# Real 2-D Fourier mixing and a sigmoid-GELU feed-forward block on one core: the Nyquist broadcast issued earlier, and VectorE's and ScalarE's work of a step in another order

## The chip, the cores and the metric

The kernel runs on one core of one Trainium2 chip. The metric is the device time of one execution in microseconds (us), of which lower is better. Before the change the median of three executions is 2043.21 us (2042.82 to 2043.45).

## The reference

```python
x        : (8, 3008, 256) float32            # batch, sequence, width
X        = fft(fft(x, axis=1), axis=2).real   # "FNet" mixing: only the real part is kept
t        = X.reshape(8 * 3008, 256)
h        = t @ w_in                           # w_in  (256, 2048)
g        = h * (1 / (1 + exp(-1.702 * h)))    # quick GELU
out      = g @ w_out                          # w_out (2048, 256)
```

The kernel folds the transform over the width (256 columns) into `w_in` once at the start. The transform over the sequence, 3008 = 47 x 64, is done in two stages on TensorE. Because the input is real, the rows come in pairs: for a frequency and its mirror image the hidden values are P + Q and P - Q (up to one column, the Nyquist column, which adds a term N of its own). So TensorE makes P and Q once and two rows of hidden values come out of them.

## The kernel before

Each batch has three blocks of frequencies, each block two halves, each half eight steps; a step takes 256 hidden units (two groups `i` of 128) for 256 (in one half of the first block 226) pairs of rows. That is 48 steps per batch and 384 in all. The first eight are treated in a simpler way; all others run through the loop below. Counted within a batch, steps 0 to 15 are block 0, 16 to 31 block 1, 32 to 47 block 2.

The loop is software-pipelined. "Step t" is one turn of it, and works on several steps at once:

```python
for t in range(n + LAG):                      # LAG = 3
    ...
    else:                                     # t >= NP = 8
        if t < n:
            if t + 2 < n:
                middle(t + 2)                 # ScalarE: g = af2 * nb            (N, needs the Nyquist broadcast)
            second(t)                         # TensorE: x[t] += Q               4 matmuls of 64 columns each
        product(t - LAG, 0)                   # TensorE: 2 of 7 output products
        if t + 1 < n:
            begin(t + 1)                      # TensorE: x[t+1] = P
        product(t - LAG, 1)                   # TensorE: the other 5 products
        ...
        if t < n:
            forward(t)                        # ScalarE: h[forward half] = gelu(x)
        sums(t - 2, nc.vector)                # VectorE: s2, s4
        if t < n:
            backward(t)                       # VectorE: h[reversed half] = g - x  (rows reversed)
            activate_back(t)                  # ScalarE: gelu of the reversed half, in place
            sums(t, nc.gpsimd)                # GpSimd:  s1, s3
    if NP <= t + 1 < n:
        doubled(t + 1)                        # VectorE: g = 2 P + N   (must be read before second(t+1) adds Q)
    ...
    if t >= LAG:
        combine(t - LAG)                      # every eighth step: finish an output block
        ...
    if t >= NP:
        spare[:] = ["b2", f"b{t % 2}"]        # PSUM banks that side work may take
    for fn, args in extra.get(t, ()):         # side work of this step, at its end
        fn(*args)
```

`x` lies in one of two PSUM banks, `b0` and `b1`, by the parity of its step. The side work borrows bank `b2` and the bank of the step that has just been turned back.

```python
def doubled(t):
    n = width(t)
    g = two(gt[t][:], n)
    nc.vector.scalar_tensor_tensor(g, two(xb[t][:], n), 2.0, g, op0=ALU.mult, op1=ALU.add)

def backward(t):
    reversed_sum(t, gt.pop(t), xb.pop(t), ALU.subtract)

def sums(t, eng):                             # h = a11, a12, a21, a22: forward 0, 1, reversed 0, 1
    ...
    if eng is nc.gpsimd:
        eng.tensor_tensor(s1, a21, a22, op=ALU.add)
        eng.tensor_tensor(s3, a11, a21, op=ALU.subtract)
    else:
        eng.tensor_tensor(s2, s1, a11, op=ALU.subtract)
        eng.tensor_tensor(s4, a12, s2, op=ALU.subtract)
```

The output products are a Strassen-Winograd scheme: seven products in place of eight, accumulated over the eight steps of a half in four PSUM banks `pot[0]`, `pot[1]`, `pot[2]` and `pot[5]`. `deep(t)` is always False in this kernel, so the parts that are guarded by it do nothing.

```python
# product(t, part): the first two of plan are part 0, the rest part 1
plan = [(0, 0, wo[:, p, 0, :], h[:, 0, 0, :n]), (0, 1, wt[:, p, 1, :], s[:, 1, :n]),
        (1, 0, wt[:, p, 2, :], s[:, 2, :n]), (1, 1, wt[:, p, 0, :], s[:, 0, :n]),
        (2, 0, wo[:, p, 3, :], s[:, 3, :n])]
if not deep(t):
    plan += [(2, 1, wo[:, p, 2, :], h[:, 0, 1, :n]), (5, 0, wt[:, p, 3, :], h[:, 1, 1, :n])]
```

After the eighth step `combine` adds the seven accumulated products up, turns the result and stores it:

```python
nc.scalar.copy(c1, pot[0][:, 0:n])
plan = [(u2, c1, m[6], ALU.add), (u3, u2, m[7], ALU.add), (u2, u2, m[5], ALU.add), (c22, u3, m[5], ALU.add),
        (c12, u2, m[3], ALU.add)]
...
plan = [*plan[:1], (c11, c1, m2, ALU.add), plan[1], plan[2], plan[4], plan[3], (c21, u3, m4, ALU.subtract)]
for out_, i0, i1, how in plan:
    nc.vector.tensor_tensor(out_, i0, i1, op=how)
    ...
for half in range(2):
    turned(t, o, half, c[:, 2 * half:])       # VectorE transpose, then four stores
```

Of the side work four kinds matter here. For every block but the first, `stage2` makes the block's `pq` (P's and Q's moving operand) in step 8 of the block before it, and `nyquist` copies the Nyquist column of `pq` to all 128 partitions by a DMA. For the next batch `fold1` (GpSimd) and `mix1` (TensorE) make the first stage in pieces, `spill` and `fill` send it through device memory, and `turn` and `load_x` bring in a later batch.

```python
def nyquist(b, blk):
    nb = nbt[b, blk] = pqp.tile([128, 512], F32, tag="nb", name="nb")   # two buffers
    row = pqt[b, blk][0:1, 1, :]
    if (b, blk) != (0, 0):
        nc.sync.dma_start(out=nb[:], in_=free(row, 0, [0, 128], [1, 512]))
        return
    ...

for b in range(B):
    t0 = b * NBLK * NF
    late = 0 if b else 3
    if b + 2 < B:
        at(t0 + 10, turn, b + 2)
    if b + 1 < B:
        for c in range(NCH):
            at(t0 + 7 + 2 * c + late, fold1, b + 1, c, nc.gpsimd)
            if c % 2:
                at(t0 + 8 + 2 * c + late, mix1, b + 1, c // 2)
        at(t0 + 24 + late, spill, b + 1)
        at(t0 + 29 + late, fill, b + 1)
        ...
    for blk in range(NBLK):
        nxt = (b, blk + 1) if blk + 1 < NBLK else (b + 1, 0)
        if nxt[0] < B:
            at(t0 + blk * NF + 8, stage2, *nxt)
            at(t0 + blk * NF + 12, nyquist, *nxt)
```

The first use of a block's broadcast is `middle(t + 2)` of the block's first step, and so stands at the head of step 14 of the block before. In the first batch GpSimd also prepares differences of the output weights (`differences`, `small_weights`) in steps 7 to 12.

Of the kernel before, what the change touches and what calls it, by code (L numbers as in the profile page):

```python
# [27 lines left out]
F32 = mybir.dt.float32  # L28
U32 = mybir.dt.uint32
ALU = mybir.AluOpType  # L30
# [13 lines left out]
LAG = 3  # L44
# [6 lines left out]
def free(ap, offset, *dims):  # L51
    return bass.AP(ap.tensor, ap.offset + offset, [list(ap.ap[0])] + [list(d) for d in dims])
# [59 lines left out]
def kernel(ctx: ExitStack, tc, x, w_in, w_out, tab1, tab2, out):  # L112
# [324 lines left out]
    def differences(n):  # L437
        ps = slice(2 * n, 2 * n + 2)
        b11, b12, b21, b22 = (wo[:, ps, q, :] for q in range(4))
        t1, t2, t3, t4 = (wt[:, ps, q, :] for q in range(4))  # L440
        for out, i0, i1 in ((t1, b12, b11), (t2, b22, t1), (t3, b22, b12), (t4, t2, b21)):
            nc.gpsimd.tensor_tensor(out, i0, i1, op=ALU.subtract)

    def fold_w(n):
# [23 lines left out]
    def width(t):  # L468

        return 226 if steps[t][1:3] == (0, 1) else 256  # L470
# [109 lines left out]
    def deep(t):  # L580

        return False
# [55 lines left out]
    def product(t, part):  # L638

        p, n = steps[t][3], width(t)  # L640
        if part == 0 and p == 0:
            for q in range(2 if t < NP else 3):
                pot[q] = bank(f"po{q}", f"o{q}")
            if t >= NP and not deep(t):
                pot[5] = bank("po5", "b2" if deep(t - 1) else "o3")
        h = ht[t]
        if t < NP:

            plan = [(half, dh, wo[:, p, 2 * f + dh, :], h[:, half, f, :n])
                    for half in range(2) for dh in range(2) for f in range(2)]  # L650
        else:
            s = st[t]
            plan = [(0, 0, wo[:, p, 0, :], h[:, 0, 0, :n]), (0, 1, wt[:, p, 1, :], s[:, 1, :n]),
                    (1, 0, wt[:, p, 2, :], s[:, 2, :n]), (1, 1, wt[:, p, 0, :], s[:, 0, :n]),
                    (2, 0, wo[:, p, 3, :], s[:, 3, :n])]
            if not deep(t):
                plan += [(2, 1, wo[:, p, 2, :], h[:, 0, 1, :n]), (5, 0, wt[:, p, 3, :], h[:, 1, 1, :n])]
        todo = plan[:2] if part == 0 else plan[2:]

        if t >= len(steps) - 2:  # L660
            if part == 0:
                return
            pot[t] = plan
            if t == len(steps) - 2:
                return
            todo = [it for both in zip(pot.pop(t - 1), pot.pop(t)) for it in both]
        begun = set() if p else pot.setdefault("begun", set())
        for q, i, lhs, rhs in todo:
            halves(pot[q][:, i * 256:i * 256 + n], lhs, rhs, start=(p == 0 and q not in begun), stop=(p == NP - 1))
            begun.add(q)  # L670
        if part and p == 0:
            del pot["begun"]

    def turned(t, o, half, src):

        b, blk, hh, p = steps[t]
        nc.vector.transpose(free(o[:], half * 512, [32, 2], [64, 8], [1, 32]), free(src, 0, [256, 2], [32, 8], [1, 32]))  # L677
        store(b, blk, hh, o, half)

    def combine(t):  # L680

        b, blk, hh, p = steps[t]
        if p < NP - 1:
            return
        n = width(t)
        o = op.tile([128, 4, 256], F32, tag="os", name="os")
        if t < NP:
            for half in range(2):
                turned(t, o, half, pot[half][:])
            return  # L690
        c = cv.tile([128, 4, 256], F32, tag="m", bufs=2, name="c")
        if n < 256:
            nc.gpsimd.memset(c[:, :, n:], 0.0)
        m = {k: pot[q][:, 256 * i:256 * i + n] for k, q, i in ((6, 0, 1), (7, 1, 0), (5, 1, 1), (3, 2, 0))}
        u2, u3 = (op.tile([128, 256], F32, tag=f"u{q}", bufs=1, name=f"u{q}")[:, :n] for q in (1, 2))
        c1 = op.tile([128, 256], F32, tag="u0", bufs=1, name="u0")[:, :n]
        nc.scalar.copy(c1, pot[0][:, 0:n])
        c11, c12, c21, c22 = (c[:, q, :n] for q in range(4))
        plan = [(u2, c1, m[6], ALU.add), (u3, u2, m[7], ALU.add), (u2, u2, m[5], ALU.add), (c22, u3, m[5], ALU.add),
                (c12, u2, m[3], ALU.add)]  # L700
        if deep(t):
            for out_, i0, i1, how in plan:
                nc.vector.tensor_tensor(out_, i0, i1, op=how)
            pot["late"] = o, c, c1, u2, u3
            return
        m2, m4 = pot[2][:, 256:256 + n], pot[5][:, 0:n]
        plan = [*plan[:1], (c11, c1, m2, ALU.add), plan[1], plan[2], plan[4], plan[3], (c21, u3, m4, ALU.subtract)]
        for out_, i0, i1, how in plan:
            nc.vector.tensor_tensor(out_, i0, i1, op=how)  # L709
            if t < len(steps) - 1:  # L710
                continue
            if out_ is c12:
                turned(t, o, 0, c[:])
            elif out_ is c22 or out_ is c21:
                i = int(out_ is c22)
                nc.vector.transpose(free(o[:], 512 + 32 * i, [64, 8], [1, 32]), free(c[:], (2 + i) * 256, [32, 8], [1, 32]))
        if t == len(steps) - 1:
            store(b, blk, hh, o, 1)
            return
        for half in range(2):  # L720
            turned(t, o, half, c[:, 2 * half:])

    def combine_small(t):

        if t < 0 or not deep(t) or steps[t][3] < NP - 1:
            return
        n, w = width(t), width(t) // 2
        o, c, c1, u2, u3 = pot.pop("late")
        d, e, other = held[3], held[3][:, 896:], u2
        nc.scalar.copy(e[:, :w], sub(1)[:, :w])  # L730

        def two_of(ap, at, by):
            return free(ap[:], at, [by, 2], [1, w])

        d22 = d[:, 256 + w:256 + 2 * w]
        for out, i0, i1 in ((two_of(d, 0, 512), free(held[3][:], 896, [0, 2], [1, w]), two_of(pot[3], 0, 128)),
                            (two_of(d, 640, 128), two_of(d, 512, 0), two_of(pot[3], 256, 128)),
                            (two_of(d, 256, w - 256), two_of(d, 640, 128), two_of(pot[4], 0, 128)),
                            (d22, d[:, 768:768 + w], sub(5)[:, :w])):
            nc.vector.tensor_tensor(out, i0, i1, op=ALU.add)  # L740
        nc.scalar.copy(other[0:64, :n], d[64:128, 0:n])
        nc.scalar.copy(d[64:128, 0:n], d[0:64, 256:256 + n])
        nc.scalar.copy(other[64:128, :n], d[64:128, 256:256 + n])
        pot["turn"] = o, c, c1, u2, u3

    def combine_last(t):

        if t < 0 or not deep(t) or steps[t][3] < NP - 1:
            return
        n = width(t)  # L750
        o, c, c1, other, u3 = pot.pop("turn")
        nc.vector.tensor_tensor(c[:, 0, :n], c1, held[3][:, 0:n], op=ALU.add)
        turned(t, o, 0, c[:])
        nc.vector.tensor_tensor(c[:, 2, :n], u3, other[:, :n], op=ALU.subtract)
        turned(t, o, 1, c[:, 2:])

    def store(b, blk, hh, o, half):

# [140 lines left out]
# [13 lines that stand above are left out]
                at(t0 + 33 + late, load_x, b + 2)  # L912
            at(t0 + 36 + late, rotate, b + 1)
        for blk in range(NBLK):
            nxt = (b, blk + 1) if blk + 1 < NBLK else (b + 1, 0)
            if nxt[0] < B:
                at(t0 + blk * NF + 8, stage2, *nxt)
                at(t0 + blk * NF + 12, nyquist, *nxt)

    for t in range(n + LAG):  # L920
        if t < NP:
# [19 lines left out]
        else:  # L941
# [11 lines left out]
                activate(t - 1)  # L953
            if t < n:
                forward(t)
            sums(t - 2, nc.vector)
            if t < n:
                backward(t)
                activate_back(t)
                sums(t, nc.gpsimd)  # L960
        if NP <= t + 1 < n:
            doubled(t + 1)
        if t >= NP:
            deeper(t - 1, 0)
            deeper(t - 2, 1)
        if t >= LAG:
            combine(t - LAG)
            combine_small(t - LAG - 1)
            combine_last(t - LAG - 2)
        if t == NP:  # L970
            held += [hp.tile(shape, F32, tag="h", name="held") for shape in
                     ([128, 2, 4, 2, 64], [128, 2, 4, 2, 64], [128, 4, 256], [128, 1024])]
# [32 lines left out]
```

## Time and profile before

| | |
|---|---|
| time, median of three | 2043.21 us |
| span of the profiled execution | 2041.2 us |
| TensorE matmuls busy | 1944.1 us (95%) |
| TensorE weight loads busy | 1295.6 us (63%) |
| VectorE busy | 1267.6 us (62%) |
| ScalarE busy | 847.7 us (42%) |
| GpSimd busy | 811.8 us (40%) |
| mean granted TensorE clock | 0.985 |
| DMA traffic over the span | 52 GB/s |

In the profile PE is a TensorE matmul, PEld its weight load, DVE is VectorE, ACT is ScalarE, POOL is GpSimd, and SP is the engine that issues the DMAs. L542 and the like are lines of the kernel: L478 is every matmul of x and of the output products, L230 `mix1`, L332 `stage2`, L346 the Nyquist broadcast, L503 `backward`, L542 `middle`, L548 `doubled`, L555 `forward`, L562 `activate_back`, L574 and L575 the sums on GpSimd, L577 and L578 those on VectorE, L709 and L677 the sums and transposes of `combine`. In a list of waits a row reads: who waited, for whom, us in total, how often, the longest. In a list by time a row reads: start, duration, engine, line, operation, what it writes and reads, how many instructions are merged in the row, and in square brackets how long the engine had been idle and what released it.

### The profile page before, as it was taken

To read this page: it belongs to the slowest core of one execution; us is meant where nothing else is said; L and a number is where in the kernel's file an instruction comes from. 1 tells how busy PE (TensorE), PEld (TensorE's weight loads), DVE (VectorE), ACT (ScalarE), POOL (GpSimd) and SP (SyncE) were. 2 spreads that over 40 slices of the span, in tenths; PEclk is the share of its full clock that TensorE was granted. 3 is DMA by queue.
4 is the path that set the end of the run, shared out by engine and by line. 5 is a ranking of instruction groups with operands and counts; after the bars stand their busy time and mean duration, and the time that the engine had idled before them with its cause. 6 is when DMAs were issued, how large, how long until landed. Compare 5 with 4: busy or idle time off the path is not lost.

```text
span 2041.2 us, 45270 instructions
## 1 busy us (share of the span) xinstructions
PE 1944.1 (95%) x19184; PEld 1295.6 (63%) x19184; DVE 1267.6 (62%) x2185; ACT 847.7 (42%) x1684; POOL 811.8 (40%) x1073
## 2 busy tenths in 40 slices
PE   8989899899999999999999999989999999998998
PEld 5666566666666666756666666666666666666665
DVE  7656566566665566755665666656666666665665
ACT  6534344444444444434443434434444444443342
POOL 4575234543345333553335523355333543232332
PEclk9999999999999999999999999999999999999999
DMA  8521440236202442116222162221720213202201
GB/s 294 124 47 32 93 51 12 47 54 106 17 14 53 73 77 17 51 17 104 46 27 47 39 101 31 18 47 41 108 26 13 17 43 56 17 12 20 22 12 22
DMA packets 145371, 104.56 MB, mean 51 GB/s; under 512 B 104914, under 2 KB 127986, under 8 KB 143984
## 3 DMA queue, kind: packets, MB, share of 16 engines
q1 hardware_dynamic: 143952, 101.14, 29.2%
q8 instruction: 150, 2.46, 0.5%
q10 hardware_dynamic: 1216, 0.52, 0.1%
q14 instruction: 53, 0.43, 0.1%
HBM read 58.38 MB, written 48.01 MB: 52 GB/s over the span
## 4 chain that ended last, share of the span: by engine, by line
PE 65%; DMA 15%; DVE 11%; SPq 3%; ACT 2%; issue 2%; POOL 1%; DVEq 0%; ACTq 0%; POOLq 0%
PE po L478 38%; PE x L478 23%; DMA nb<-pq 11%; DVE os L677 2%; DVE c L709 2%; DVE h L503 2%; SPq L769 2%; PE ps L230 1%; DVE u L709 1%; PE ps L332 1%; DVE g L548 1%; DMA xt<-in_x_dram 1%; DMA t<-Td 1%; DMA xt<-Xr 1%; DVE s L578 1%
## 5 line engine op out<-in xcount | busy, mean ns | idle before, releaser
L478 PE MATMUL x<-pq,wcs 128*64 128x256 f32 (+1 forms) x6016 | 780.7, 381 | 49.1 <-DVE g L548 49.1
L478 PE MATMUL po<-h,wo 128*64 128x256 f32 (+1 forms) x4768 | 638.3, 377 | 0.0
L478 PEld LDWEIGHTS x<-pq,wcs 128*64 128x64 f32 x6016 | 428.1, 138 | 282.2 <-DVE g L548 72.1
L478 PE MATMUL po<-s,wo 128*64 128x256 f32 (+1 forms) x4512 | 575.6, 376 | 0.0
L503 DVE TENSOR_TENSOR h<-g,x 128x512 f32<-128x512 f32 (+2 forms) x440 | 258.1, 599 | 506.7 <-ACT h L555 506.2
L574 POOL TENSOR_TENSOR s<-h 128x256 f32<-128x256 f32 (+1 forms) x282 | 204.3, 724 | 780.6 <-ACT h L562 773.9
L555 ACT ACTIVATE h<-x 128x512 f32<-128x512 f32 (+1 forms) x376 | 220.8, 587 | 551.8 <-PE x L478 516.1
L478 PEld LDWEIGHTS po<-h,wo 128*64 128x64 f32 x4768 | 347.9, 138 | 159.9 <-issue 0.4
L478 PEld LDWEIGHTS po<-s,wo 128*64 128x64 f32 x4512 | 327.2, 138 | 153.8 <-issue 1.1
L542 ACT ACTIVATE g<-nb,af 128x256 f32<-128x256 f32 (+1 forms) x752 | 333.7, 492 | 146.2 <-DMA nb<-pq 145.4
L562 ACT ACTIVATE h<-h 128x512 f32<-128x512 f32 (+1 forms) x376 | 233.8, 622 | 376.5 <-DVE h L503 376.5
L548 DVE SCALAR_TENSOR_TENSOR g<-x,g 128x512 f32<-128x512 f32 (+1 forms) x376 | 255.3, 679 | 108.5 <-PE x L478 108.4
L575 POOL TENSOR_TENSOR s<-h 128x256 f32<-128x256 f32 (+1 forms) x282 | 238.0, 844 | 0.0
L578 DVE TENSOR_TENSOR s<-h,s 128x256 f32<-128x256 f32 (+1 forms) x282 | 212.2, 752 | 9.7
L574 POOL TENSOR_TENSOR held<-h 128x256 f32<-128x256 f32 (+1 forms) x94 | 68.6, 730 | 374.8 <-ACT h L562 366.9
L478 PE MATMUL po<-held,wo 128*64 128x256 f32 (+1 forms) x1504 | 192.1, 375 | 0.0
L577 DVE TENSOR_TENSOR s<-s,h 128x256 f32<-128x256 f32 (+1 forms) x282 | 166.9, 592 | 0.7 <-POOL s L574 0.7
L478 PEld LDWEIGHTS po<-held,wo 128*64 128x64 f32 x1504 | 109.6, 137 | 49.9
L709 DVE TENSOR_TENSOR c<-u,po 128x256 f32<-128x256 f32 (+1 forms) x188 | 69.8, 412 | 34.0 <-PE po L478 32.4
L575 POOL TENSOR_TENSOR held<-h 128x256 f32<-128x256 f32 (+1 forms) x94 | 82.7, 880 | 0.0
L577 DVE TENSOR_TENSOR held<-held,h 128x256 f32<-128x256 f32 (+1 forms) x94 | 75.1, 799 | 4.2 <-POOL held L574 4.2
L230 PE MATMUL ps<-xt,w 47*64 47x256 f32 x434 | 42.6, 430 | 33.1 <-DVE h L503 27.2
(88 smaller groups left out, 831.1 us busy)
## 6 DMA issues: line engine op xcount, KB each, us to landing
out_dram<-os SPq DMA_DIRECT2D x284, 64.0 KB
Td<-xt SPq DMA_DIRECT2D x14, 768.0 KB
t<-Td SPq DMA_DIRECT2D x7, 1536.0 KB
xt<-in_x_dram SPq DMA_DIRECT2D x14, 512.0 KB
xt<-Xr SPq DMA_DIRECT2D x14, 512.0 KB
nb<-pq SPq DMA_DIRECT2D x23, 256.0 KB
out_dram<-os SPq DMA_DIRECT2D x96, 56.0 KB
Xr<-in_x_dram SPq DMA_DIRECT2D x7, 752.0 KB
```

Of the source, the lines that this page charges most:

```text
L230: nc.tensor.matmul(o, lhsT=w, rhs=rhs, start=first, stop=end)
L478: nc.tensor.matmul(out[c0:c0 + 64], lhsT=lhs[:, c0:c0 + 64], rhs=rhs, skip_group_check=True, **how)
L503: nc.vector.tensor_tensor(free(h[:], 512 + at + m - 1, [256, 2], [RUN, blocks], [-1, m]), *ins, op=op)
L542: nc.scalar.activation(g[:, i * 256:i * 256 + n], nbt[b, blk][:, hh * 256:hh * 256 + n], ACTF.Copy, scale=af2[:, f:f + 1])
L548: nc.vector.scalar_tensor_tensor(g, two(xb[t][:], n), 2.0, g, op0=ALU.mult, op1=ALU.add)
L555: nc.scalar.activation(two(h[:], n), two(xb[t][:], n), ACTF.Gelu_apprx_sigmoid)
L562: nc.scalar.activation(g, g, ACTF.Gelu_apprx_sigmoid)
L574: eng.tensor_tensor(s1, a21, a22, op=ALU.add)
L575: eng.tensor_tensor(s3, a11, a21, op=ALU.subtract)
L577: eng.tensor_tensor(s2, s1, a11, op=ALU.subtract)
L578: eng.tensor_tensor(s4, a12, s2, op=ALU.subtract)
L709: nc.vector.tensor_tensor(out_, i0, i1, op=how)
```

## The change

There are four parts.

1. The Nyquist broadcast is issued in step 9 of a block, one step behind `stage2`, not in step 12.
2. VectorE's order in a step becomes: reversed rows (`backward`), 2P + N (`doubled`), then the two sums. Before, the sums came first.
3. The reversed half of step t - 1 is activated in step t, right behind the forward half of step t, and GpSimd's sums of it follow a step later too. The product that needs only GpSimd's s3 moves forward to second place in the plan, ahead of the one that needs s2.
4. `combine` adds two of its results in one instruction of double width, and turns each half of the result as soon as it is complete. For this one product keeps its opposite sign (the difference of weights is taken the other way round), and the three scratch tiles become one. The special order for the very last block is gone.

It is for taking waits out of TensorE's path: those for the broadcast, and those for VectorE.

```diff
-        for out, i0, i1 in ((t1, b12, b11), (t2, b22, t1), (t3, b22, b12), (t4, t2, b21)):
+        for out, i0, i1 in ((t1, b12, b11), (t2, b22, t1), (t3, b22, b12), (t4, b21, t2)):
@@
-            plan = [(0, 0, wo[:, p, 0, :], h[:, 0, 0, :n]), (0, 1, wt[:, p, 1, :], s[:, 1, :n]),
-                    (1, 0, wt[:, p, 2, :], s[:, 2, :n]), (1, 1, wt[:, p, 0, :], s[:, 0, :n]),
+            plan = [(0, 0, wo[:, p, 0, :], h[:, 0, 0, :n]), (1, 0, wt[:, p, 2, :], s[:, 2, :n]),
+                    (0, 1, wt[:, p, 1, :], s[:, 1, :n]), (1, 1, wt[:, p, 0, :], s[:, 0, :n]),
                     (2, 0, wo[:, p, 3, :], s[:, 3, :n])]
@@ combine
-        u2, u3 = (op.tile([128, 256], F32, tag=f"u{q}", bufs=1, name=f"u{q}")[:, :n] for q in (1, 2))
-        c1 = op.tile([128, 256], F32, tag="u0", bufs=1, name="u0")[:, :n]
+        u = op.tile([128, 3, 256], F32, tag="u", bufs=1, name="u")
+        c1, u2, u3 = (u[:, q, :n] for q in range(3))
         nc.scalar.copy(c1, pot[0][:, 0:n])
...
+        m5 = free(pot[1][:], 256, [0, 2], [1, n])
+        plan = [(u2, c1, m[6], ALU.add), (u3, u2, m[7], ALU.add),
+                (free(c[:], 256, [512, 2], [1, n]), u[:, 1:3, :n], m5, ALU.add),
+                (c[:, 1, :n], c[:, 1, :n], m[3], ALU.add)]
         for out_, i0, i1, how in plan:
             nc.vector.tensor_tensor(out_, i0, i1, op=how)
...
+        for out_, i0, i1, i in ((c[:, 0, :n], c1, pot[2][:, 256:256 + n], 0), (c[:, 2, :n], u3, pot[5][:, 0:n], 1)):
+            nc.vector.tensor_tensor(out_, i0, i1, op=ALU.add)
+            turned(t, o, i, c[:, 2 * i:])
@@
                 at(t0 + blk * NF + 8, stage2, *nxt)
-                at(t0 + blk * NF + 12, nyquist, *nxt)
+                at(t0 + blk * NF + 9, nyquist, *nxt)
@@ the loop
             if t < n:
                 forward(t)
-            sums(t - 2, nc.vector)
+            if NP < t <= n:
+                activate_back(t - 1)
+                sums(t - 1, nc.gpsimd)
             if t < n:
                 backward(t)
-                activate_back(t)
-                sums(t, nc.gpsimd)
         if NP <= t + 1 < n:
             doubled(t + 1)
         if t >= NP:
+            sums(t - 2, nc.vector)
...
```

The diff is cut to what acts. The parts behind `deep(t)` change as well, but are not run in either kernel.

More of the change, by code (lines that the diff above doesn't have):

```diff
@@ L694, in combine @@
         m = {k: pot[q][:, 256 * i:256 * i + n] for k, q, i in ((6, 0, 1), (7, 1, 0), (5, 1, 1), (3, 2, 0))}
-        u2, u3 = (op.tile([128, 256], F32, tag=f"u{q}", bufs=1, name=f"u{q}")[:, :n] for q in (1, 2))
-        c1 = op.tile([128, 256], F32, tag="u0", bufs=1, name="u0")[:, :n]
+        u = op.tile([128, 3, 256], F32, tag="u", bufs=1, name="u")
+        c1, u2, u3 = (u[:, q, :n] for q in range(3))
         nc.scalar.copy(c1, pot[0][:, 0:n])
[L698 to L707, printed above, removed]
+        m5 = free(pot[1][:], 256, [0, 2], [1, n])
+        plan = [(u2, c1, m[6], ALU.add), (u3, u2, m[7], ALU.add),
+                (free(c[:], 256, [512, 2], [1, n]), u[:, 1:3, :n], m5, ALU.add),
+                (c[:, 1, :n], c[:, 1, :n], m[3], ALU.add)]
         for out_, i0, i1, how in plan:
             nc.vector.tensor_tensor(out_, i0, i1, op=how)
[L710 to L718, printed above, removed]
+        pot["late"] = o, c, u
+        if deep(t):
             return
-        for half in range(2):
-            turned(t, o, half, c[:, 2 * half:])
+        for out_, i0, i1, i in ((c[:, 0, :n], c1, pot[2][:, 256:256 + n], 0), (c[:, 2, :n], u3, pot[5][:, 0:n], 1)):
+            nc.vector.tensor_tensor(out_, i0, i1, op=ALU.add)
+            turned(t, o, i, c[:, 2 * i:])
     def combine_small(t):
@@ L726, in combine_small @@
             return
[L727 to L730, printed above, removed]
+        n, w, d = width(t), width(t) // 2, held[3]
+        e, saved = d[:, 896:896 + w], d[:, 768:]
         def two_of(ap, at, by):
             return free(ap[:], at, [by, 2], [1, w])
+        nc.scalar.copy(e, sub(1)[:, :w])
         d22 = d[:, 256 + w:256 + 2 * w]
-        for out, i0, i1 in ((two_of(d, 0, 512), free(held[3][:], 896, [0, 2], [1, w]), two_of(pot[3], 0, 128)),
+        for out, i0, i1 in ((two_of(d, 0, 512), two_of(d, 896, 0), two_of(pot[3], 0, 128)),
                             (two_of(d, 640, 128), two_of(d, 512, 0), two_of(pot[3], 256, 128)),
@@ L740, in combine_small, with combine_last @@
             nc.vector.tensor_tensor(out, i0, i1, op=ALU.add)
[L741 to L746, printed above, removed]
+        nc.scalar.copy(saved[64:128, :n], d[0:64, 256:256 + n])
+        nc.scalar.copy(d[0:64, 256:256 + n], d[64:128, 0:n])
+        nc.scalar.copy(d[64:128, 0:n], saved[64:128, :n])
+    def combine_last(t, half):
         if t < 0 or not deep(t) or steps[t][3] < NP - 1:
@@ L750, in combine_last @@
         n = width(t)
[L751 to L755, printed above, removed]
+        o, c, u = pot["late"]
+        if half == 0:
+            nc.vector.tensor_tensor(free(c[:], 0, [512, 2], [1, n]), free(u[:], 0, [512, 2], [1, n]),
+                                    free(held[3][:], 0, [256, 2], [1, n]), op=ALU.add)
+        turned(t, o, half, c[:, 2 * half:])
     def store(b, blk, hh, o, half):
@@ L963 @@
         if t >= NP:
-            deeper(t - 1, 0)
-            deeper(t - 2, 1)
+            sums(t - 2, nc.vector)
+            deeper(t - 2, 0)
+            deeper(t - 3, 1)
         if t >= LAG:
@@ L968 @@
             combine_small(t - LAG - 1)
-            combine_last(t - LAG - 2)
+            combine_last(t - LAG - 2, 0)
+            combine_last(t - LAG - 3, 1)
         if t == NP:
```

## The prediction

> **What bounds the kernel now.** I read the page's busy times first, then the list of waits, then instructions by time around the two waits that stand out, then the granted clock there.
>
> ```profile
> PE   1944.1 (95%) x19184; PEld 1295.6 (63%) x19184; DVE 1267.6 (62%) x2185; ACT 847.7 (42%) x1684; POOL 811.8 (40%) x1073
> ```
>
> TensorE is the bound; no other engine comes near it. The change takes no matmul away, so it can win only what TensorE stands still (2041.2 - 1944.1 = 97 us, some 10 of them before the first matmul and after the last) and what slow-clock matmuls cost. The list of waits says for whom it stands still:
>
> ```profile
> ACT g L542 <- DMA nb<-pq: 145.4, 22, 10.0
> PE x L478 <- DVE g L548: 49.1, 51, 5.6
> PE ps L230 <- DVE h L503: 27.2, 6, 5.9
> PE ps L230 <- POOL xt L206: 5.9, 1, 5.9
> ```
>
> TensorE never waits for the broadcast itself; ScalarE does, 22 of 23 times, 6.6 us on average, and TensorE's rows name VectorE. One place by time, around step 14 of the fourth batch, shows how the one becomes the other:
>
> ```profile
> 863.65 0.55 SPq L346 DMA_DIRECT2D nb<-pq  x1
> ...
> 871.43 0.65 PE L230 MATMUL ps<-xt,w 47*64 47x256 f32 x4
> 874.89 0.91 ACT L542 ACTIVATE g<-nb,af 128x256 f32<-128x256 f32 x2 [9.08 <-DMA nb<-pq]
> 875.70 0.52 ACT L555 ACTIVATE h<-x 128x452 f32<-128x452 f32 x1
> 876.26 0.69 DVE L503 TENSOR_TENSOR h<-g,x 128x448 f32<-128x448 f32 x2 [8.68 <-ACT h L555]
> ...
> 877.09 1.97 PE L230 MATMUL ps<-xt,w 47*64 47x256 f32 x12 [5.01 <-DVE h L503]
> ```
>
> `middle` stands first in ScalarE's step, so `forward` queues behind the broadcast, `backward` behind `forward`, and the x bank that `mix1` borrows comes free only after `backward`. Where there is no side work, `doubled` is last in that chain and TensorE waits at x.
>
> The second wait is behind each `combine`. One place, step 27 of the same batch:
>
> ```profile
> 938.97 0.42 DVE L709 TENSOR_TENSOR c<-u,po 128x256 f32<-128x256 f32 x1 [0.71 <-PE po L478]
> ...
> 943.79 0.68 DVE L548 SCALAR_TENSOR_TENSOR g<-x,g 128x512 f32<-128x512 f32 x1
> ...
> 944.53 1.08 PE L478 MATMUL x<-pq,wcs 128*64 128x256 f32 x8 [0.42 <-DVE g L548]
> ```
>
> VectorE idles 0.71 us for the fourth product of the list, then works without a break to the end of `doubled`, 0.43 us too late.
>
> Last, the clock (columns: stretch, length, busy us and instructions of the five engines, granted clock, DMA):
>
> ```profile
> 866.40:870.60 4.20, 4.20 (x48) 3.16 (x46) 1.15 (x2) 0.00 (x0) 3.92 (x6) 1.00 1.03 155
> 877.00:879.00 2.00, 1.91 (x13) 0.86 (x14) 1.52 (x3) 1.14 (x2) 1.36 (x2) 0.50 0.04 8
> 879.00:881.00 2.00, 2.00 (x14) 1.30 (x14) 0.00 (x0) 1.57 (x4) 0.08 (x1) 0.50 0.00 0
> ```
>
> For about 4 us after the gap TensorE runs at half clock. A long gap costs more than its length.
>
> [...] 0.50 after 5.01 us of idling, 1.00 again at 885.5. [...] the first VectorE sum took 0.38 us at 942.44, with GpSimd idle, and 0.85 us at 822.51, beside GpSimd's sums. [...]
>
> **Part 1, the broadcast.** The transposes that make `pq` in this batch end at 845.27 (start 843.83, 1.44 us). Nothing else is then in SP's stream until the stores at 855.7, so the new issue falls at about 845.4, not 863.65. How long does it take? Issued at 863.65 behind `turn`, it let ScalarE go at 874.84, 11.2 us; the next one, with no `turn`, was issued at 945.86 and its packets ran from 947.0 to 957.1. So it lands at about 857, and step 14 wants it at 865.8 (ScalarE's idle time began 9.08 us before 874.89): 9 us to spare. In block 1 the transposes end at 931.2, `spill`'s packets are through by about 931, the broadcast lands at about 942 and is wanted at 952.4: 10 us to spare. I expect no wait for it anywhere.
>
> What that is worth I take from the length of each step in the trace, first matmul of `second` to the next: TensorE's order makes it very regular. An undisturbed step is 4.75 us (four stretches 0.86 + 0.86 + 0.86 + 2.16), 4.20 where all parts are 226 wide; a `mix1` piece adds 1.12, and the step after side work is 0.05 longer. In the fourth batch steps 14 and 15 last 11.86 + 5.43 us against 4.20 + 1.12 and 4.30 + 0.05, an excess of 7.6. Done so for every batch:
>
> Steps 14 and 15, second to eighth batch: 8.8, 7.0, 7.6, 7.5, 9.9, 4.3, 7.2; sum 52.2 (with rounding).
> Steps 30 and 31, all batches: 7.2, 2.5, 1.4, 1.4, 3.1, 1.5, 2.4, 1.7; sum 21.2.
> Step 46, first seven: 1.1, 1.7, 1.1, 1.1, 2.8, 1.4, 2.0; sum 11.2.
>
> Together 84.6 us. The first batch's steps 13 and 14 hold another 9.1 us that I do not count: its gap of 5.93 us ends at GpSimd (the fourth wait above), which there does the weight differences, two pieces of `fold1` and four sums from 98.5 to 125.0 with hardly a pause. Under the new order the sums in that run begin with step 8's, at about 97.75 (after `forward` of step 9, 96.54 + 0.55, plus 0.58), 0.75 us earlier, so about 0.8 comes back. Part 1: 85.4 us.
>
> **Parts 2 and 4, behind `combine`.** The 0.43 us gap makes step 3, 27, 35 or 43 last 5.34 us and the next 4.80, against 4.75 each: 0.64 lost, 31 times, 19.8 us. Three places in steps 11 and 19 add 2.7; 22.5 us in all. Between the end of `doubled` (937.94) and the latest end of the next one that costs nothing (944.07, which is the observed 944.47 less 0.4) VectorE has 6.1 us. Before, it had the work of `combine`, two sums, `backward` and `doubled`, 5.9 us, plus the 0.71 of idling. The new order puts the two sums ahead of `combine`, where they fill that idle time; the accumulations are then complete when they are asked for. Against it, the sums now meet the end of GpSimd's (which shift to about 2.2 to 3.9 us after the step's start; `doubled` ends at 3.45), so the first may take 0.4 to 0.5 us in place of 0.32, and the later instructions meet GpSimd's next pair. The double-width add replaces two adds of 0.41 by one of about 0.69 (as `backward`, 128x512), a gain of 0.1. My sum is 6.0 to 6.4 us against 6.1, so a gap of 0 to 0.3 stays. A new wait is near: the product now second in the plan writes `pot[1]` in the next step's part 0, 1.29 us after that step starts (940.5), and the double-width add must have read it: 937.94 + two sums 0.9 + three adds 0.41 + 0.41 + 0.69 = 940.35. Just enough. I count 10 of the 22.5 us.
>
> **Part 3** moves ScalarE's 0.63 us forward, because it no longer waits for `backward`, and delays the result by most of a step. Products use it three steps later, and s3 is ready a step before. In plain steps ScalarE, VectorE (3.0 us of 4.75) and GpSimd (1.6) are off the path: 0.
>
> **The end.** The special order for the last block is gone: after the last product one add (0.41) and one full transpose (0.65) in place of add and half transpose (0.45): 0.2 to 0.3 us lost.
>
> Sum: 85.4 + 10 - 0.3 = 95 us; 2043.2 - 95 = 1948 us.
>
> **Rivals.** (a) The broadcast stays late, because something ahead of it in SP's stream holds it up, or it is slower beside `spill`. For: it is slow (256 KB in 10 us), and in block 1 it comes right behind 1.5 MB of `spill`. Against: the margins of 9 to 10 us. If block 1 kept its waits, 21 us would be missing: about 1969. (b) VectorE behind `combine` becomes the wait: the new early use of `pot[1]` and the sums ahead of `combine` make the gap larger, say 0.8 us at 47 places; then 10 us gained become some 15 lost: about 1973. For: it fits by only 0.15 us. Against: the removed 0.71 us of idling, and fewer sums beside GpSimd. (c) Both waits go entirely, and the first batch's with them: 84.6 + 9.1 + 22.5, about 1927. Against it stands GpSimd's unbroken run. (d) The gaps at step 14 hid a late `fold1`. Before, `fold1` ended at 870.47 and `mix1` began at 871.43; GpSimd's sums start earlier now, so this does not bind.
>
> **Range and chances.** Part 1 rests on observed step lengths and wide margins, perhaps -10 to +8 us; the `combine` part is worth 0 to 20. That gives 1936 to 1962. The 2% limit is at 2002 us, which would need half of part 1 to fail: 0.96 faster, 0.03 same, 0.01 slower.
>
> **What would show it.** Right: ScalarE's row for nb gone from the waits; TensorE's rows for `backward` and most of that for `doubled` gone; mean clock above 0.985, near 0.995; one gap of about 5 us left near 120 us; steps 14, 30 and 46 as long as their undisturbed neighbours; TensorE busy at 98% or more; the sums on VectorE shorter than their 592 and 752 ns. Wrong: a row of po waiting for the adds of `combine` (b), ScalarE still released by the broadcast (a), or the 5 us gap gone (c).

## The result, and the profile after

The changed kernel takes 1957.29 us (median of four runs, 1955.58 to 1959.08), the kernel before 2043.01 us beside it: a ratio of 0.958, 95% interval 0.957 to 0.960. The prediction was 1948 us, range 1936 to 1962.

The first line of the page and TensorE's list of waits, both of the changed kernel:

```profile
PE 1927.6 (99%) x19184; PEld 1300.1 (66%) x19184; DVE 1180.0 (60%) x2137; ACT 808.1 (41%) x1684; POOL 780.4 (40%) x1073
```

```profile
PE ps L230 <- POOL xt L206: 4.1, 1, 4.1
...
PE x L478 <- DVE g L548: 1.6, 3, 0.8
...
PE po L478 <- DVE c L703: 1.5, 3, 0.6
```

Line numbers are the changed kernel's from here on: L703 and L708 are the adds of `combine`, L755 its stores (L769 in the kernel before), L338 the transposes that make `pq`, L206 the last piece of `fold1`, L182 `load_x`, L312 `fill`. The row of `mix1` behind `backward` (27.2 us before) is gone. `doubled` (49.1 before) seems almost gone too, and a new row has come, po behind the adds of `combine`, rival (b)'s sign. Both rows count only three of these waits; step lengths will show more. What remains of any size is the first batch's gap at GpSimd. The group of `middle` (columns: busy us, mean ns, idle us before it and what ended it) says what became of the broadcast: it waited 145.4 us before, and now

```profile
L542 ACT ACTIVATE g<-nb,af 128x256 f32<-128x256 f32 (+1 forms) x752 | 334.7, 496 | 0.8 <-DVE h L512 0.8
```

The mean granted clock went from 0.985 to 0.998. Measured as in the prediction, first matmul of `second` to the next, the two traces differ by these sums (us, negative is faster):

| where | predicted | changed kernel | broadcast alone | 
|---|---|---|---|
| steps 14, 15 of the second to eighth batch | -52.2 | -52.2 | -52.2 |
| steps 30, 31 | -21.2 | -21.7 | -21.7 |
| steps 46, 47 | -11.2 | -11.6 | -11.6 |
| first batch, steps 13, 14 | -0.8 | -0.4 | +0.6 |
| steps behind `combine` and the next | -10 | +0.9 | 0.0 |

"Broadcast alone" is the first experiment below. Two more terms complete the changed kernel: the first of these steps begins 1.57 us later in its profile (90.86 for 89.29 us), and from the last one's first matmul to the end it takes 19.0 us in place of 20.1. The spans differ by 84.3 us: 85.4 + 0.4 - 0.9 - 1.6 + 1.1 = 84.4.

So the broadcast's share came as worked out, and the steps behind `combine` did not get shorter at all. Here is the same step 27 of the fourth batch in the changed kernel, by time:

```profile
900.24 0.69 DVE L548 SCALAR_TENSOR_TENSOR g<-x,g 128x512 f32<-128x512 f32 x1 [0.28 <-PE x L478]
...
900.58 0.73 POOL L575 TENSOR_TENSOR s<-h 128x256 f32<-128x256 f32 x1
...
900.84 0.75 DVE L577 TENSOR_TENSOR s<-s,h 128x256 f32<-128x256 f32 x1
...
902.18 1.03 PE L478 MATMUL x<-pq,wcs 128*64 128x256 f32 x8
...
902.94 0.69 DVE L703 TENSOR_TENSOR c<-u,po 128x512 f32<-128x512 f32 x1
...
903.04 0.60 PE L478 MATMUL po<-h,wo 128*64 128x256 f32 x4
...
903.78 0.65 PE L478 MATMUL po<-s,wo 128*64 128x256 f32 x4
...
906.78 0.68 DVE L548 SCALAR_TENSOR_TENSOR g<-x,g 128x512 f32<-128x512 f32 x1
...
907.51 1.08 PE L478 MATMUL x<-pq,wcs 128*64 128x256 f32 x8
```

The step lasts 907.51 - 902.18 = 5.33 us; before it was 5.34. TensorE now loses time twice: 0.31 us at the second product (it should start 0.43 us after 903.04, and starts only after the double-width add has ended, at 903.63), and the rest before x at 907.51. VectorE works without a break from the end of one `doubled` (900.93) to the end of the next (907.46), 6.53 us. In the kernel before it was 937.94 to 944.47, 6.53 us as well, of which it stood idle for 0.71.

### The profile page after: what moved, and what is told of

Its sections match the earlier page's. It is cut to its first block, busy times and chain, and to the rows that moved or that the text cites. A ratio compares the mean times of both kernels' runs of the same rounds, so it can differ in the third digit from the quotient of the medians.

```text
span 1956.9 us, 45607 instructions
## 1 busy us (share of the span) xinstructions
PE 1927.6 (99%) x19184; PEld 1300.1 (66%) x19184; DVE 1180.0 (60%) x2137; ACT 808.1 (41%) x1684; POOL 780.4 (40%) x1073
## 4 chain that ended last, share of the span: by engine, by line
PE 83%; DVE 12%; DMA 2%; issue 1%; POOL 1%; ACT 1%; DVEq 0%; SPq 0%; POOLq 0%; ACTq 0%
PE po L478 48%; PE x L478 30%; DVE os L677 2%; DVE g L548 2%; PE ps L230 2%; DVE c L703 1%; PE ps L332 1%; DVE u L703 1%; DVE c L708 1%; DVE s L577 1%; DVE h L503 1%; DVE s L578 1%; DMA raw<-in_moe_w_in_dram 1%; DMA nb<-pq 1%; PE psw L448 0%
## 5 line engine op out<-in xcount | busy, mean ns | idle before, releaser
L478 PE MATMUL x<-pq,wcs 128*64 128x256 f32 (+1 forms) x6016 | 772.6, 377 | 3.7 <-DVE g L548 1.6
L574 POOL TENSOR_TENSOR s<-h 128x256 f32<-128x256 f32 (+1 forms) x282 | 203.3, 721 | 853.8 <-issue 632.0
L575 POOL TENSOR_TENSOR s<-h 128x256 f32<-128x256 f32 (+1 forms) x282 | 207.6, 736 | 0.0
L577 DVE TENSOR_TENSOR s<-s,h 128x256 f32<-128x256 f32 (+1 forms) x282 | 188.1, 667 | 2.3 <-POOL s L574 2.3
L574 POOL TENSOR_TENSOR held<-h 128x256 f32<-128x256 f32 (+1 forms) x94 | 69.6, 741 | 249.7 <-ACT h L562 159.2
L578 DVE TENSOR_TENSOR s<-h,s 128x256 f32<-128x256 f32 (+1 forms) x282 | 139.1, 493 | 9.7
L203 POOL TENSOR_TENSOR xt<-xt 111x510 f32<-111x510 f32 x56 | 77.1, 1377 | 4.4
L575 POOL TENSOR_TENSOR held<-h 128x256 f32<-128x256 f32 (+1 forms) x94 | 71.4, 759 | 0.0
L677 DVE STREAM_TRANSPOSE os<-c 128x512 f32<-128x512 f32 x94 | 66.9, 712 | 3.8
L233 ACT COPY xt<-ps 128x512 f32<-128x512 f32 x56 | 30.1, 589 | 94.2 <-PE ps L230 84.5
```

The costliest lines, as they stand in the source:

```text
L203: eng.tensor_tensor(low, low, free(t, up + D - 1, [-D, 2], [-1, D - 1]), op=ALU.add)
L478: nc.tensor.matmul(out[c0:c0 + 64], lhsT=lhs[:, c0:c0 + 64], rhs=rhs, skip_group_check=True, **how)
```

## The experiments

Each theory's numbers were written before its run. Ratios are to the kernel before on the same chip; the intervals are 95%. The kernel before took 2043.0 to 2045.7 us beside the different groups of runs, so times of two groups compare to some 3 us only; step lengths in the traces are sharper.

### Is the gain the broadcast alone, or does it need the new order?

```diff
  # kernel before; and the same line the other way in the changed kernel
-                at(t0 + blk * NF + 12, nyquist, *nxt)
+                at(t0 + blk * NF + 9, nyquist, *nxt)
```

Expected of the kernel before with this line alone:

> The kernel before with one line changed: the Nyquist broadcast issued in step 9, not 12. Theory A (the whole gain is the broadcast; the new order of VectorE, ScalarE and combine is worth nothing, because the steps behind combine last 5.34 us in both kernels): 1957 to 1960 us, 84 us under the kernel before, no TensorE gap at steps 14, 30 and 46, gaps of 0.43 us behind combine as before. Theory B (the gain needs both, the new order lets ScalarE and VectorE catch up): 1970 to 2000 us, with part of the gaps at steps 14 and 30 still there.

Measured: 1958.67 us, ratio 0.957 (0.956 to 0.959), against 0.958 for the whole change. TensorE's waits in it:

```profile
PE x L478 <- DVE g L548: 16.0, 35, 0.9
PE ps L230 <- POOL xt L206: 5.9, 1, 5.9
```

The 35 waits behind `combine` and the first batch's gap are as in the kernel before; all else of the 49.1 us row has gone. One line is worth the whole gain: theory A.

Expected of the changed kernel without it:

> The changed kernel with the broadcast back in step 12; all else of the change kept. Theory A: the new order gains nothing by itself, 2036 to 2044 us, gaps of 1 to 5 us at steps 14, 30 and 46 as before. Theory B (the new order alone makes the kernel more tolerant of a late broadcast): 2000 to 2025 us.

Measured: 2052.84 us, ratio 1.004 (1.003 to 1.006): not only no gain, a small loss, 7 us against the kernel before. It is outside theory A's numbers, in the other direction from B. ScalarE waits 169.3 us for the broadcast here (145.4 before). By step lengths the steps of the first three rows of the table are 11.8 us longer than in the kernel before. Why a late broadcast costs the new order more was not followed up.

### Why was step 12 late, and step 9 not?

```diff
-                at(t0 + blk * NF + 9, nyquist, *nxt)
+                at(t0 + blk * NF + 10, nyquist, *nxt)
```

> The changed kernel with the broadcast in step 10, where in block 0 of the first six batches it stands behind that step's turn (1.5 MB between two places in device memory) and behind the stores of combine. Theory A1 (being ahead of turn is what counts in block 0; SP runs ahead of TensorE, so steps 10 and 12 give the same issue time there): blocks 1 and 2 have no wait left, but steps 14 and 15 of the second to sixth batch keep nearly all of their 40.8 us excess: 1995 to 2000 us. Theory A2 (what counts is the lead in steps, and one step later costs nothing because 9 us were to spare): 1957 to 1960 us.

Measured: 2047.95 us, ratio 1.002 (1.001 to 1.003). Both theories failed: one step later, and the gain is gone in all three blocks. SP's instructions by time show why, at block 1 of the fourth batch (the first of the two transposes whose result is stored here starts at 944.90):

```profile
945.64 3.89 SPq L755 DMA_DIRECT2D out_dram<-os  x8
949.57 0.53 SPq L346 DMA_DIRECT2D nb<-pq  x1
950.20 0.54 SPq L312 DMA_DIRECT2D t<-Td  x1
```

The same place in the changed kernel, with the transposes that make `pq`:

```profile
892.74 1.44 DVE L338 STREAM_TRANSPOSE pq<-ps 128x256 f32<-128x256 f32 x4 [1.56 <-PE ps L332]
...
894.21 0.55 SPq L346 DMA_DIRECT2D nb<-pq  x1
905.26 3.89 SPq L755 DMA_DIRECT2D out_dram<-os  x8
909.25 0.41 SPq L312 DMA_DIRECT2D t<-Td  x1
```

And in the kernel before, with the broadcast in step 12:

```profile
941.95 3.87 SPq L769 DMA_DIRECT2D out_dram<-os  x8
945.86 0.53 SPq L346 DMA_DIRECT2D nb<-pq  x1
```

`combine` falls in steps 2 and 10 of every block, and its stores come before the side work of its step. A broadcast in step 10 or 12 stands behind these stores in SP's stream (eight in blocks 1 and 2, twelve and `turn` in block 0), and these wait for a transpose that VectorE does a step later. So "step 10" and "step 12" are the same instant, the end of the stores, and step 9 is the last place in front of them. From the end of the transposes that make `pq` to the issue, in the fourth batch:

| | block 0 | block 1 | block 2 |
|---|---|---|---|
| before, step 12 | 18.4 us | 14.7 us | 14.7 us |
| changed, step 10 | 19.3 us | 15.0 us | 15.0 us |
| changed, step 9 | under 0.1 us | under 0.1 us | under 0.1 us |

That gives theory A3: it is the place in SP's stream. Its test is to send the step-10 broadcast from another queue, where no stores are in front of it:

```diff
-        nc.sync.dma_start(out=nb[:], in_=free(row, 0, [0, 128], [1, 512]))
+        nc.scalar.dma_start(out=nb[:], in_=free(row, 0, [0, 128], [1, 512]))
```

> The changed kernel with the broadcast in step 10 again, but issued from ScalarE's DMA queue, not SP's. Theory A3 (what makes the broadcast late is its place in SP's stream: behind the stores of combine, which wait for the transposes of the next step, and in block 0 behind turn): it goes out at the end of step 10, some 8 us before SP would have sent it, and no wait for it is left in blocks 1 and 2; in block 0 it shares the DMA engines with turn from another queue and is at most 2 us late. 1957 to 1970 us. Theory A2' (one step of delay by itself uses up the margin): 2040 to 2050 us, as from SP's queue.

Measured: 1962.99 us, ratio 0.960 (0.959 to 0.962). It goes out 6.5 us after `pq` is ready in most of blocks 1 and 2 and 9.4 us in most of block 0, and ScalarE's wait has shrunk to six pieces, from 165.1 us with SP's queue:

```profile
ACT g L542 <- DMA nb<-pq: 6.6, 6, 1.2
```

All six lie in step 14, of the second to seventh batch. Theory A3 holds; steps 14, 30 and 46 are as long as in the changed kernel in every batch after the first. Of the 5.7 us more than the changed kernel, 4.9 lie in the first batch, where GpSimd's first `fold1` stands still for 8.05 us and steps 13 and 14 take 23.2 us in place of 18.3. It waits for a load of `xt`: SP sends the last two of the eight only from 113.55 us on, where the kernel before had sent them by 69.2. SP's own list of waits names what it waited for:

```profile
SPq L182 <- DMA nb<-pq: 45.3, 1, 45.3
```

By this row the load waits until this broadcast (issued at 102.3) has landed: it starts at 113.55, 11.2 us after that issue. Why it has to wait for it is not shown. So sending the broadcast from the other queue costs something here that has nothing to do with step 10.

### What keeps the steps behind combine at 5.33 us?

Theory C: VectorE's unbroken run from one `doubled` to the next, 6.53 us, sets the step. Rival D: the new wait for `pot[1]` does. The first run takes D's cause away:

```diff
-  plan = [(0, 0, wo.., h..), (1, 0, wt[:, p, 2, :], s[:, 2, :n]),
-          (0, 1, wt[:, p, 1, :], s[:, 1, :n]), (1, 1, ...),
+  plan = [(0, 0, wo.., h..), (0, 1, wt[:, p, 1, :], s[:, 1, :n]),
+          (1, 0, wt[:, p, 2, :], s[:, 2, :n]), (1, 1, ...),
```

> The changed kernel with the old order of products, so that part 0 of the step behind combine writes pot[0] twice and no longer pot[1]. In the changed kernel TensorE waits there twice: some 0.3 us at the second product for the double-width add, and some 0.3 us at x for doubled. Theory C (VectorE's unbroken run from one doubled to the next, 6.5 us, sets the length of the step; the first wait only takes place of the second): the first wait goes, the second grows to about 0.4 to 0.5 us, the steps still last 5.3 us, 1955 to 1959 us. Theory D (the new wait at pot[1] costs by itself): the step falls to about 5.05 us, 10 to 14 us less in all, 1943 to 1948 us.

Measured: 1957.51 us, ratio 0.957 (0.956 to 0.959). One place by time:

```profile
905.72 1.03 PE L478 MATMUL x<-pq,wcs 128*64 128x256 f32 x8
...
907.01 0.60 PE L478 MATMUL po<-s,wo 128*64 128x256 f32 x4
...
910.31 0.68 DVE L548 SCALAR_TENSOR_TENSOR g<-x,g 128x512 f32<-128x512 f32 x1
...
911.05 1.08 PE L478 MATMUL x<-pq,wcs 128*64 128x256 f32 x8 [0.41 <-DVE g L548]
```

The second product no longer waits (907.01 is 1.29 us after the step's start, as it should be), the wait at x has grown to 0.41, and the step is 911.05 - 905.72 = 5.33 us again. The wait has only moved. The second run shortens VectorE's run instead, by putting one 0.71 us transpose behind the next step's sums; the third does both:

```diff
   nc.vector.tensor_tensor(out_, i0, i1, op=ALU.add)
-  turned(t, o, i, c[:, 2 * i:])
+  if i == 0 or t == len(steps) - 1:
+      turned(t, o, i, c[:, 2 * i:])
+
+def second_half(t):
+    if NP <= t < len(steps) - 1 and steps[t][3] == NP - 1:
+        o, c, _ = pot["late"]
+        turned(t, o, 1, c[:, 2:])
 ...
   combine(t - LAG)
+  second_half(t - LAG - 1)
```

> The changed kernel, but the transpose and the stores of the second half of each result (but the last) are put into the next step, behind its sums. That takes 0.7 us out of VectorE's run from one doubled to the next (6.5 us, of which about 6.1 cost nothing). Theory C (that run sets the step behind combine): the wait at x goes; what stays is the wait of the second product for the double-width add, about 0.3 us, so those steps last 5.0 to 5.1 us in place of 5.33: about 9 us less, 1945 to 1950 us. Theory D (only the wait at pot[1] counts): nothing changes, 1955 to 1959 us.

> Both at once: the second half's transpose a step later, and the old order of products, so that part 0 does not write pot[1]. Theory C: no wait is left behind combine, those steps fall to 4.75 to 4.80 us, 0.6 us at some 34 places: about 20 us less than the changed kernel, 1935 to 1940 us. Theory D: as without it, since the old order alone gained nothing: 1955 to 1959 us.

Measured: 1946.47 us, ratio 0.952 (0.950 to 0.953) with the transpose moved; 1934.57 us, ratio 0.946 (0.945 to 0.948) with both. The steps behind `combine` last 5.08 us and 4.75 us. The first time lies in theory C's range and the second 0.4 us below it, both step lengths are C's, and D is refuted in its strong form: the wait at `pot[1]` counts, but only once VectorE is no longer later than it. One place of the last kernel:

```profile
890.78 1.03 PE L478 MATMUL x<-pq,wcs 128*64 128x256 f32 x8
...
892.07 0.60 PE L478 MATMUL po<-s,wo 128*64 128x256 f32 x4
...
894.66 0.68 DVE L548 SCALAR_TENSOR_TENSOR g<-x,g 128x512 f32<-128x512 f32 x1
...
895.52 1.03 PE L478 MATMUL x<-pq,wcs 128*64 128x256 f32 x8
...
896.04 0.70 DVE L677 STREAM_TRANSPOSE os<-c 128x512 f32<-128x512 f32 x1
```

`doubled` ends at 895.34, x starts at 895.52, a full-speed step of 4.74 us after 890.78; the transpose follows behind, where nobody waits.

Is the new order needed for that? The kernel before got the early broadcast and the late second transpose, and kept all its old orders:

```diff
   # kernel before, broadcast in step 9
-  for half in range(2):
-      turned(t, o, half, c[:, 2 * half:])
+  turned(t, o, 0, c[:])
+  ...                      # turned(t, o, 1, c[:, 2:]) in the next step, as above
```

> The kernel before with the broadcast in step 9 and the second half's transpose and stores a step later; the old orders of VectorE, ScalarE, products and combine are kept. Theory C (only the length of VectorE's run from one doubled to the next matters): 0.7 us less than the 6.6 of the kernel before, against some 6.1 that cost nothing, so the steps behind combine fall to about 4.75 to 4.85 us: 1937 to 1943 us, as good as the changed kernel with the same step. Theory G (the new order is needed for it): 1950 to 1960 us.

Measured: 1939.27 us, ratio 0.948 (0.947 to 0.950). Steps behind `combine` mostly at 4.75, as theory C has it. The new order is not needed for it. The 1934.57 us of the new order are 4.7 us less, but the intervals of the two ratios overlap. In the two profiles the span differs by 5.2 us: the start (the first of these steps begins at 88.3 us there and 91.1 here), the end (19.0 and 20.1 us) and 0.05 us in most of the second steps behind `combine`. The start cannot be put down to the order: among the nine profiles of the changed kernel and its variants it falls anywhere between 88.3 and 95.4 us.

### The first batch's gap

`small_weights` makes tables on GpSimd that only the inactive parts read, in the kernel before as well. Leaving it out leaves the output as it is:

```diff
-        at(9 + i, small_weights, i)
```

> The changed kernel without small_weights, whose 16 instructions of 0.45 to 0.6 us on GpSimd in steps 9 to 12 of the first batch make tables that nothing reads here. Theory E (the first batch's gap near 125 us is GpSimd being behind with fold1): fold1 is done some 8 us earlier, the gap goes, steps 13 and 14 fall from 11.55 + 6.78 to about 5.32 + 4.25 us: 1947 to 1950 us. Rival F (the gap is the first piece of mix1 waiting for its x data): the gap moves by less than 1 us, 1956 to 1959 us.

Measured: 1950.43 us, ratio 0.954 (0.952 to 0.956). The last piece of the second `fold1` before `mix1`, in the changed kernel and then without `small_weights`:

```profile
124.81 0.72 POOL L206 TENSOR_TENSOR xt<-xt 111x254 f32<-111x254 f32 x1
```

```profile
118.21 0.72 POOL L206 TENSOR_TENSOR xt<-xt 111x254 f32<-111x254 f32 x1
```

6.6 us earlier, TensorE's row for it is gone, and steps 13 and 14 take 5.77 + 4.25 in place of 11.55 + 6.78 us: 8.3 us less, of which the two medians show 6.9. That is theory E, although the time lies 0.4 us above its range and `fold1` came 6.6 us earlier, not 8; F is refuted.

### All of it

> The second half a step later, the old order of products, and no small_weights. If theories C and E hold and the waits are independent: 1957 - 20 - 9 = 1928 us (1924 to 1932). If one gain hides the other: about 1937.

Measured: 1927.58 us, ratio 0.943 (0.941 to 0.944). The gains add up, 22.3 and 8.3 us against the changed kernel by step lengths, and it is faster than both kernels. In its trace TensorE has no wait over 0.8 us after the first 50 us.

## Why the prediction was right, and where it was off

**The broadcast** was right in its size to 1%: predicted 84.6 us, measured 85.4 by step lengths, and the experiment with that line alone gives the whole gain. The issue came where I put it, less than 0.1 us after `pq` was ready, and no wait was left. The clock part of it was right too, since part of the 85.4 us is no gap at all: in these steps the pauses between TensorE's matmuls fell from 60.2 us to none. My estimate for the slow clock, TensorE's busy time there times the share of the clock that was not granted, is 18.5 us; 6.7 us are in neither. What I had not seen is why step 12 was late. I took the issue time of the kernel before as it was and did not ask what stood in front of it beyond `turn`; the run at step 10 showed that it was the stores. The prediction did not need it, but going by the lead in steps (theory A2) I would have called step 10 safe, and it is worth nothing.

**Behind `combine`** the prediction failed in size: 10 us counted, -0.9 measured. The mechanism is the one written down (VectorE's run between two `doubled`, and the add that must have read `pot[1]`), but terms of the sum were mis-sized. The time that costs nothing is not 6.1 us: I took the gap of 0.43 us off the observed end, where the step was 0.59 us too long, so it is about 5.95. The experiments bear that out: with the old orders and the late transpose the run is 5.94 us, `doubled` ends just in time, and the step lasts 4.75. The run of the changed kernel is not 6.0 to 6.4 us but 6.53. The old work in it was 5.82 us (6.53 - 0.71), not 5.9, so the removed idling of 0.71 us is paid back in full. The two sums take 1.11 us (0.68 + 0.43 in the chain) in place of 0.74 in the old order and the 0.9 I allowed. The first of them now runs beside GpSimd's second sum, 900.58 to 901.31, and there takes 0.75 us (0.68 in the chain); with GpSimd idle the same add took 0.40 at 907.38 in this trace and 0.38 at 942.44 in the kernel before. What makes it longer beside GpSimd is not shown. I had expected both sums to be shorter on average; the second is (493 ns for 752), the first became longer (667 for 592). The rest is two transposes, 1.42 us in the chain where they stood at 1.21 when they followed each other, and small pauses between the adds. And the margin of 0.15 us at `pot[1]` became a wait of 0.31. So rival (b)'s wait came, but it cost nothing, since it lies inside the other. That the total stayed in the range is due to the range, which allowed for no gain here.

**The first batch** gave 0.4 us, not 0.8. **The end** was expected 0.3 us longer and is 1.1 us shorter. The old list of adds had an add that waits for the last products in second place and held the others up behind it; now three instructions come before the first that waits for them, and VectorE finishes 1.7 us after the last product, where it took 3.2. **The start** is 1.6 us later in this pair of profiles, which is within what it varies by.

By the two traces the prediction was -85.4 - 10 + 0.3 = -95.1, the measurement -85.4 - 0.4 + 0.9 - 1.1 + 1.6 = -84.4. The 10.9 us missed behind `combine` are the whole distance; the other differences cancel.

## What to carry to other kernels

In these runs a DMA was issued when everything before it in its engine's stream had been released, not in the step it is written in (behind the stores 14.7 to 19.3 us after its data was ready, in front of them under 0.1 us): look for the stores in front of it, and put a transfer that others need ahead of stores that nobody waits for. When two engines' waits overlap, shorten the unbroken run of the one that finishes last; taking only the other wait away, or reordering within that run, gained nothing here (5.33 us a step each time, against 5.34 before). The length of a step, from one fixed instruction to the next, is a better measure of a wait than the gap in it, since it also holds what comes with the gap: the clock (in the kernel before 0.50 from 877 to 881 us, behind the gap of 5.01 us, and 0.98 from there to 885.5) and the matmuls that start late.

## What the runs showed of the hardware that I had not expected

The list of waits shows 1.6 and 1.5 us for the two waits behind `combine` in the changed kernel, while those steps lose 0.58 us each at some 30 places: where a wait is split in two short ones, most of it is in no row. Nor do the pauses between matmuls show it. In the steps behind `combine` and the next they fell from 15.2 to 8.5 us, although these steps became 0.9 us longer. And the broadcast of 256 KB from one partition, whose packets ran from 947.0 to 957.1 us in the kernel before (26 GB/s, the engines 87.7% busy), is slow. It needs 11.2 us from issue to use, so of the 20.5 us between its data being ready (845.27) and its use (865.8) some 9 are left for waiting in a queue.
